# A cross-attention and maxout kernel: the order of its prologue, with state 1's small load and products placed later

## The chip, the cores and the metric

The kernel runs on one core of one Trainium2 chip. The metric is device time in microseconds (us) of one execution; lower is better. The kernel before takes 147.46 us (median of three runs, 147.34 to 148.67).

## The reference

Two parts follow each other. The first is attention between a sequence `x` (8 states in the batch, 8 heads, 512 rows, 64 columns) and a small `state` (32 rows per head), in both directions:

```python
scores = scale * x @ state.T ;  a = softmax(scores) ;  xread = a @ state
scores2 = scale * state @ x.T ; a2 = softmax(scores2); sread = a2 @ x
x = concat([xread, sread], axis=2)      # 544 rows per state, heads side by side: 512 columns
```

The second is a maxout layer over all 4352 rows: `g = maximum(x @ w1, x @ w2)`, `out = g @ w_out`, with `w1` and `w2` of 512 x 1024 and `w_out` of 1024 x 512, all in float32.

## The kernel before, in words

The work goes state by state (b = 0 to 7, one per batch element). The kernel uses `maximum(h1, h2) = h2 + relu(h1 - h2)`, so that it needs only the difference `wd` = W1 - W2 and the product `wwo` = W2 Wo. It also folds the state S into the weights: S (W1 - W2) and S W2 Wo together are a tile `sw` per state. The rows of one state are then `relu(a S (W1-W2)) Wo + a S W2 Wo`: "l1" (L348) multiplies `sw` with the transposed attention weights `aT` and takes relu, "l2" (L361, L366) multiplies the result with `wo` and adds the second term. All products are in bf16, so each float32 load is cast first.

From state 2 on, a loop (L550) issues the states one after another. All that comes before, states 0 and 1 with the load and preparation of the weights, is the prologue. Its order on every engine is written out by hand in the string `ORDER` (L18): tokens are read from left to right (L544), and each issues one step. Since every engine works through its own instructions in the order of issue, the string sets the queue of each engine. A token is of one of three kinds:

- A bare name is a DMA on SP's queue: `ldx.b.g` loads half of x of state b (512 KB, L134), `ldw1.q` and `ldw2.q` a quarter of W1 or W2 (512 KB, L145), `ldwo.f0.f1` two of eight rows of tiles of Wo (512 KB, L150), `ldS.lo.hi` states lo to hi (64 KB for one state, L155; state 0's load goes to ACT's queue instead, L451). `atd.b`, `xtd.b` and `std` are DMAs that transpose within the chip's memory: of the attention weights (L270), of x (L214) and of states 3 to 7 (L172). `store.b` writes an output.
- A name with `:n` is a group of matmuls of TensorE into PSUM bank n. `idle.9.512:7` issues nine matmuls on zeros (L446). `S.lo.hi` transposes the state (two transposes for one state, L176), `xt.b.k` a quarter of x (four, L219), `w2.q` a quarter of W2 (eight, L419), `at.b.g` half of the attention weights (four, L274). `sc.b.h` are scores (eight, L228), `sr.b` is the read of the state's side (32 small ones, L284), `ww.i.f0.f1` are two of the eight products of row i of W2 Wo (L439). `swh.b.z` is S times columns 512z to 512z + 511 of `wd` or `wwo` (eight, into two banks, L315). `sw` is the same for a quarter. `l1.b.f` are two matmuls (L348), `l2p` and `l2o` parts of l2 (L501, L505).
- A name with `>A`, `>V` or `>P` is a step of ScalarE (ACT), VectorE (DVE) or GpSimd (POOL). `cS`, `ce`, `cb`, `cw2`, `cwo` are casts of the state, of x (in two layouts), of W2 and of Wo (L160, L195, L201, L415, L436). `sub.q.k` is one eighth of W1 - W2 (L431). `cSm` are masked casts of states 2 to 7 (L165). `red` and `nm` sum and normalise (L250, L254). A name that also occurs as a matmul group moves that group's result out of PSUM, on lines 92 (ACT), 94 (DVE) and 96 (POOL), or 342 and 344 for relu.

A copy or cast helper has one line for all tiles, so an instruction is told by its tile. The float32 tiles `h` that loads write to rotate over ten buffers (L121). SP allows eight of its transfers to be under way; the next one waits for the one that was issued eight before it.

Of the kernel before, what the change touches and what calls it, by code (L numbers as in the profile page):

```python
# [15 lines left out]


ORDER = """  # L18
ldx.0.1 ldx.0.0 ldw2.1 ldwo.0.2 ldS.1.2 ldw2.0 ldw1.0 ldw1.1 ldwo.2.4 ldx.1.1 ldw2.3 ldw2.2 ldwo.4.6 ldwo.6.8
ldw1.2 ldw1.3 ldx.1.0 ldx.2.1 ldx.2.0 ldS.2.8 idle.9.512:7 cS.0.1>V ce.0.2>V S.0.1:0 S.0.1.0>A ce.0.3>P xt.0.2:1  # L20
S.0.1.1>A xt.0.2>V xt.0.3:7 ce.0.0>V ce.0.1>A xt.0.3>V xt.0.0:3 xt.0.1:4 xt.0.0>A sc.0.1:5 xt.0.1>V sc.0.1>A
sc.0.0:6 cw2.1>V sc.0.0>A red.0.1>V w2.1:2 sr.0:0 w2.1>A cwo.0>P red.0.0>V cS.1.2>A sr.0>V nm.0.1>P ww.2.0.2:1
cw2.0>A S.1.2:7 ww.3.0.2:3 nm.0.0>V S.1.2.0>A w2.0:4 S.1.2.1>A sub.0.0>V at.0.0:5 w2.0>A at.0.1:6 sub.0.1>V
sub.1.1>V at.0.0>A ww.1.0.2:2 ww.0.0.2:0 at.0.1>A sub.1.0>V cwo.1>V swh.0.0:7,4 swh.1.0:5,6 swh.0.0.1>A swh.0.0.0>V
ww.1.2.4:2 swh.1.0.1>A ww.0.2.4:0 swh.1.0.0>V l1.0.0:4 l1.0.3:7 l1.0.0>A l1.0.2:6 ce.1.2>V l1.0.1:5 ce.1.3>P
l1.0.3>V l1.0.2>A xt.1.2:4 ww.2.2.4:1 l1.0.1>A xt.1.2>V cw2.3>P xt.1.3:7 ww.3.2.4:3 xt.1.3>V l2p.0.1.0.2:6 w2.3:4
cw2.2>P sc.1.1:5 w2.3>V l2p.0.3.0.2:7 sc.1.1>A l2p.0.3.2.4:7 red.1.1>V w2.2:4 l2p.0.1.2.4:6 w2.2>A l2p.0.0.0.2:5
cwo.2>V l2p.0.0.2.4:5 nm.1.1>V cwo.3>A ww.2.4.6:1 ww.0.4.6:0 ww.3.4.6:3 sub.2.1>V ww.3.6.8:3 sub.2.0>V ww.0.6.8:0
ww.3>A ww.2.6.8:1 sub.3.1>V ww.0>A ww.1.4.6:2 ww.1.6.8:2 sub.3.0>V ww.2>A l2p.0.2.0.2:4 ww.1>A ce.1.0>V swh.0.1:3,0
ce.1.1>P l2p.0.2.2.4:4 swh.0.1.1>A swh.0.1.0>V xt.1.0:1 xt.1.1:2 xt.1.0>A l1.0.5:0 xt.1.1>V cb.2.1>P l1.0.4:3  # L30
l1.0.5>A sc.1.0:1 l1.0.4>V l1.0.6:2 ce.2.3>P sc.1.0>A l1.0.7:0 ce.2.1>P l1.0.6>A red.1.0>V l2p.0.0.4.6:5
l2p.0.1.4.6:6 ce.2.2>P l1.0.7>A sw.0.4:3,1 nm.1.0>P cSm.1>A l2p.0.3.4.6:7 sw.0.4.1>V l2p.0.0.6.8:5 l2p.0.1.6.8:6
sw.0.4.0>A ce.2.0>P atd.1 l2p.0.3.6.8:7 cSm.0>A cb.2.0>P l2o.0.1:6 swh.1.2:2,0 l2.0.1>V swh.1.1:1,3 xtd.2 std
ldx.3.0 ldx.3.1 swh.1.2.0>A l2o.0.3:7 swh.1.1.0>V S.2.3:6 swh.1.2.1>A l2o.0.0:5 S2>V l2p.0.2.4.6:4 l2.0.3>A
l2.0.0>V l2p.0.2.6.8:4 swh.1.1.1>A l1.1.2:2 l1.1.3:1 l1.1.2>V l1.1.0:0 l1.1.3>A l1.1.4:6 l1.1.0>A l1.1.7:7 l1.1.1:5
l1.1.4>A l1.1.7>V l1.1.5:3 l1.1.1>A l1.1.6:2 l1.1.5>V sc.2.0:1 l1.1.6>A sc.2.1:0 l2o.0.2:4 sc.2.0>A l2.1.0:6
sc.2.1>A red.2.0>V l2.0.2>A store.0 red.2.1>V nm.2.0>P l2.1.1:7 l2.1.0>A nm.2.1>P atd.2 l2.1.1>A
"""


# [688 lines left out]
```

## Time and profile before

| what | value |
|---|---|
| runs | 147.34, 147.46, 148.67 us |
| the execution that was profiled | 148.65 us |
| its span, from the first to the last instruction | 146.9 us |
| busy: TensorE, its weight loads, DVE, ACT, POOL | 137.7, 67.2, 80.0, 70.0, 47.6 us |
| read from memory and written to it | 15.20 MB, 8.91 MB |

A row of the timeline has the start in us from the span's start, the duration, the engine, the line, the operation, its output and inputs, their shapes and the number of instructions that were merged; the bracket gives the idle time of the engine before it and what ended it. PE is TensorE, PEld its weight loads, SPq the issue of a DMA by SP. Matmuls are pipelined: one of 512 columns has a duration of about 0.38 us, and the next starts 0.216 us after it, so a group of n takes n x 0.216 of TensorE's time. A row of stretches gives, for each, the busy time of PE, PEld, DVE, ACT and POOL with the number of instructions in parentheses, then the granted clock, the busy share of the DMA engines and GB/s. In the DMA view, q1 is the queue of the kernel's transfers and q8 one that fetches instructions; its share is that of 16 DMA engines over the stretch asked for.

### The profile page before, as it was taken

Reading aid. Unit: us, or ns where it says so; the run is one execution under the profiler, and the core shown is the slowest. Engines: PE = TensorE matmul, PEld = TensorE weight load, DVE = VectorE, ACT = ScalarE, POOL = GpSimd, SP = SyncE. Lnnn points to the kernel's source line nnn. Section 1 sums busy time; section 2 is a strip of 40 time slices with the busy share of each in tenths; the row PEclk is TensorE's granted clock in tenths of the full one; section 3 lists DMA queues with packets and bytes.
Section 4 is the critical chain, followed back from the end, with each engine's and each line's share of the span. In section 5 each row is a group of like instructions: output and inputs, shape, how many; then the busy total and the mean of one; then the engine's idle time right before and its main releaser. Section 6 shows DMA issues by size and latency. Waiting matters only on the chain. (4 is left out here: it accounts for less than half of the span.)

```text
span 146.9 us, 3048 instructions
## 1 busy us (share of the span) xinstructions
PE 137.7 (94%) x1218; PEld 67.2 (46%) x1218; DVE 80.0 (54%) x159; ACT 70.0 (48%) x133; POOL 47.6 (32%) x73
## 2 busy tenths in 40 slices
PE   6857599999999999999999999999999999999991
PEld 2444156453454445444544454454445344753451
DVE  1586568764663838463854585276637485720321
ACT  4388346687782556336541835181547145510200
POOL 4233060277008806464390457056500500000000
PEclk9999999999999999999999999999999999999998
DMA  4999999932999999996989685879307032400524
GB/s 106 334 375 388 367 389 370 331 61 47 200 266 350 185 270 355 152 230 261 184 167 267 274 165 113 269 286 147 71 2 288 0 71 107 185 9 9 189 97 143
DMA packets 36979, 29.68 MB, mean 202 GB/s; under 512 B 23904, under 2 KB 32352, under 8 KB 36064
## 3 DMA queue, kind: packets, MB, share of 16 engines
q1 hardware_dynamic: 36688, 29.36, 69.7%
q8 instruction: 11, 0.18, 0.5%
q10 hardware_dynamic: 272, 0.07, 0.2%
q14 instruction: 8, 0.07, 0.2%
HBM read 15.20 MB, written 8.91 MB: 164 GB/s over the span
## 5 line engine op out<-in xcount | busy, mean ns | idle before, releaser
L368 PE MATMUL bank<-wo,r 128*128 128x512 bf16 (+2 forms) x264 | 61.5, 373 | 0.1
L368 PEld LDWEIGHTS <-r 128*128 128x128 bf16 x264 | 25.4, 98 | 29.5 <-issue 1.1
L92 ACT COPY h<-bank 128x512 f32<-128x512 f32 (+1 forms) x17 | 9.7, 573 | 48.9 <-PE bank L368 48.9
L344 DVE TENSOR_SCALAR r<-bank 128x512 bf16<-128x512 f32 x29 | 20.1, 692 | 18.6 <-PE bank L353 18.1
L353 PE MATMUL bank<-aT,sw 128*128 128x512 bf16 x128 | 29.3, 379 | 0.0
L342 ACT ACTIVATE r<-bank 128x512 bf16<-128x512 f32 x35 | 20.7, 611 | 7.2 <-PE bank L353 6.7
L255 POOL TENSOR_TENSOR a<-e,er 128x512 bf16<-128x512 bf16 x14 | 14.9, 1082 | 26.7 <-ACT e L247 16.4
L94 DVE CAST sw<-bank 128x512 bf16<-128x512 f32 x23 | 14.7, 685 | 13.1 <-PE bank L323 13.1
L96 POOL CAST xe<-h 128x512 bf16<-128x512 f32 x27 | 16.2, 634 | 16.6 <-DMA h<-in_x_dram 14.4
L363 PE MATMUL bank<-sw,aT 128*128 128x512 bf16 (+2 forms) x66 | 19.1, 374 | 0.0
L96 POOL CAST xb<-h 128x1024 bf16<-128x1024 f32 x12 | 12.3, 1042 | 19.5 <-issue 12.5
L353 PEld LDWEIGHTS <-sw 128*128 128x128 bf16 x128 | 12.1, 98 | 13.7
L94 DVE COPY h<-bank 128x512 f32<-128x512 f32 (+1 forms) x16 | 10.5, 661 | 11.8 <-PE bank L368 10.2
L92 ACT CAST sw<-bank 128x512 bf16<-128x512 f32 x25 | 13.4, 600 | 2.0 <-PE bank L323 2.0
L251 DVE TENSOR_REDUCE sums<-e 128x16 f32<-128x512 bf16 x16 | 10.6, 664 | 2.5 <-ACT e L247 2.3
L441 PE MATMUL bank<-wo,w2t 128*128 128x512 bf16 x32 | 8.0, 379 | 3.3 <-DVE wo L94 1.7
L247 ACT ACTIVATE e<-bank 128x512 bf16<-128x512 f32 x16 | 8.9, 596 | 2.4 <-PE bank L239 1.8
L363 PEld LDWEIGHTS <-aT 128*128 128x128 bf16 x66 | 5.4, 98 | 5.0 <-issue 0.7
L239 PEld LDWEIGHTS <-xt 128*128 128x128 bf16 x128 | 5.0, 98 | 2.0 <-ACT xt L92 0.3
L433 DVE TENSOR_TENSOR wd<-h,h 128x512 bf16<-128x512 f32 x8 | 5.1, 688 | 1.3 <-DMA h<-in_moe_w_dram 1.3
L441 PEld LDWEIGHTS <-w2t 128*128 128x128 bf16 x32 | 2.9, 97 | 6.2 <-issue 2.1
L239 PE MATMUL bank<-sbd,xt 128*128 128x64 bf16 x128 | 5.4, 193 | 0.2 <-ACT xt L92 0.2
(75 smaller groups left out, 99.7 us busy)
## 6 DMA issues: line engine op xcount, KB each, us to landing
out_dram<-h SPq DMA_DIRECT2D x7, 1024.0 KB, 4.5
h<-in_x_dram SPq DMA_DIRECT2D x10, 512.0 KB, 5.3
h<-in_moe_w_dram SPq DMA_DIRECT2D x8, 512.0 KB, 10.3
h<-in_x_dram SPq DMA_DIRECT2D x3, 1024.0 KB, 5.8
h<-in_moe_w_out_dram SPq DMA_DIRECT2D x4, 512.0 KB, 11.5
out_dram<-h SPq DMA_DIRECT2D x3, 256.0 KB, 2.4
out_dram<-rs SPq DMA_DIRECT2D x2, 256.0 KB, 2.4
sf<-in_state_dram SPq DMA_DIRECT2D x1, 384.0 KB, 9.2
```

The source lines that it names most:

```text
L92: nc.scalar.copy(o, i)
L94: nc.vector.tensor_copy(o, i)
L96: nc.gpsimd.tensor_copy(o, i)
L239: nc.tensor.matmul(pv[:, c, kk], d["xt"][:, c, k, :], sbd[:, b, k, :], start=(c == 0 and kk == 0), stop=(c == NC - 1 and kk == 1))
L251: nc.vector.tensor_reduce(es_all[:, b, hh], e_view(b, hh), axis=AXX, op=ALU.add)
L255: (nc.gpsimd if eng == "P" else nc.vector).tensor_mul(e_view(b, hh, "a"), e_view(b, hh), d_(b)["er"][:, hh].unsqueeze(3).to_broadcast([128 ...
L342: nc.scalar.activation(out=o, in_=p, func=ACTF.Relu)
L344: nc.vector.tensor_scalar(o, p, scalar1=0.0, scalar2=None, op0=ALU.max)
L353: nc.tensor.matmul(p, SW[b][:, g, f * 128:(f + 1) * 128], AT[b][:, g].rearrange("p c t -> p (c t)"), start=(g == 0), stop=(g == 1))
L363: nc.tensor.matmul(p[:, lo:hi], AT[b][:, g, c, :], SW[b][:, g, FF + lo:FF + hi], start=(start and g == 0), stop=(stop and g == 1))
L368: nc.tensor.matmul(p[:, lo:hi], R[b][:, f, c * 128:(c + 1) * 128], wo[:, f, lo:hi], start=(start and j == 0), stop=(stop and j == len(fs) ...
L441: nc.tensor.matmul(p, w2t[:, f, i, :], wo[:, f, :], start=(f == 0), stop=(f == NF - 1))
```

## The change

Only `ORDER` differs. In the prologue's first part:

- `ldS.1.2` goes from behind `ldwo.0.2` to behind `ldwo.2.4` in SP's queue, so behind two quarters of W1, one of W2 and the second Wo piece. Its cast `cS.1.2`, its transposes `S.1.2` and the first group `swh.1.0` of state 1 move too: before, they were issued between the first ww groups and ahead of the second Wo piece's cast; now they follow it (`cwo.1>V swh.0.0 cS.1.2>A swh.0.0.0>A ... S.1.2:4 ww.3.2.4 ww.0.2.4 ... l1.0.1 swh.1.0`).
- `idle.9` becomes `idle.8`.
- The early casts and evictions change engines: `cS.0.1` from DVE to ACT, `ce.0.3` from POOL to DVE, `ce.0.0` from DVE to POOL, `ce.0.1` from ACT to DVE, `cw2.1` from DVE to POOL, `nm.0.1` from POOL to DVE; state 0's first scores `sc.0.1` go ahead of the transposes of x's other half.
- Banks and the order of the later groups change up to the prologue's end. `std` goes behind `ldx.3.0` and `ldx.3.1`, the masked casts `cSm` go from ACT to DVE, `nm.1.0` from POOL to DVE, and `S.2.3` from ahead of state 1's l1 groups to among them.

```diff
 ORDER = """
-ldx.0.1 ldx.0.0 ldw2.1 ldwo.0.2 ldS.1.2 ldw2.0 ldw1.0 ldw1.1 ldwo.2.4 ldx.1.1 ldw2.3 ldw2.2 ldwo.4.6 ldwo.6.8
-ldw1.2 ldw1.3 ldx.1.0 ldx.2.1 ldx.2.0 ldS.2.8 idle.9.512:7 cS.0.1>V ce.0.2>V S.0.1:0 S.0.1.0>A ce.0.3>P xt.0.2:1
-S.0.1.1>A xt.0.2>V xt.0.3:7 ce.0.0>V ce.0.1>A xt.0.3>V xt.0.0:3 xt.0.1:4 xt.0.0>A sc.0.1:5 xt.0.1>V sc.0.1>A
-sc.0.0:6 cw2.1>V sc.0.0>A red.0.1>V w2.1:2 sr.0:0 w2.1>A cwo.0>P red.0.0>V cS.1.2>A sr.0>V nm.0.1>P ww.2.0.2:1
-cw2.0>A S.1.2:7 ww.3.0.2:3 nm.0.0>V S.1.2.0>A w2.0:4 S.1.2.1>A sub.0.0>V at.0.0:5 w2.0>A at.0.1:6 sub.0.1>V
-sub.1.1>V at.0.0>A ww.1.0.2:2 ww.0.0.2:0 at.0.1>A sub.1.0>V cwo.1>V swh.0.0:7,4 swh.1.0:5,6 swh.0.0.1>A swh.0.0.0>V
-ww.1.2.4:2 swh.1.0.1>A ww.0.2.4:0 swh.1.0.0>V l1.0.0:4 l1.0.3:7 l1.0.0>A l1.0.2:6 ce.1.2>V l1.0.1:5 ce.1.3>P
-l1.0.3>V l1.0.2>A xt.1.2:4 ww.2.2.4:1 l1.0.1>A xt.1.2>V cw2.3>P xt.1.3:7 ww.3.2.4:3 xt.1.3>V l2p.0.1.0.2:6 w2.3:4
...
-l1.0.5>A sc.1.0:1 l1.0.4>V l1.0.6:2 ce.2.3>P sc.1.0>A l1.0.7:0 ce.2.1>P l1.0.6>A red.1.0>V l2p.0.0.4.6:5
-l2p.0.1.4.6:6 ce.2.2>P l1.0.7>A sw.0.4:3,1 nm.1.0>P cSm.1>A l2p.0.3.4.6:7 sw.0.4.1>V l2p.0.0.6.8:5 l2p.0.1.6.8:6
-sw.0.4.0>A ce.2.0>P atd.1 l2p.0.3.6.8:7 cSm.0>A cb.2.0>P l2o.0.1:6 swh.1.2:2,0 l2.0.1>V swh.1.1:1,3 xtd.2 std
-ldx.3.0 ldx.3.1 swh.1.2.0>A l2o.0.3:7 swh.1.1.0>V S.2.3:6 swh.1.2.1>A l2o.0.0:5 S2>V l2p.0.2.4.6:4 l2.0.3>A
...
+ldx.0.1 ldx.0.0 ldw2.1 ldwo.0.2 ldw2.0 ldw1.0 ldw1.1 ldwo.2.4 ldS.1.2 ldx.1.1 ldw2.3 ldw2.2 ldwo.4.6 ldwo.6.8
+ldw1.2 ldw1.3 ldx.1.0 ldx.2.1 ldx.2.0 ldS.2.8 idle.8.512:7 cS.0.1>A ce.0.2>V S.0.1:0 ce.0.3>V xt.0.2:1 S.0.1.0>V
+xt.0.3:2 xt.0.2>A S.0.1.1>V xt.0.3>V ce.0.0>P sc.0.1:6 ce.0.1>V xt.0.0:4 sc.0.1>A xt.0.1:7 xt.0.0>V xt.0.1>A
+red.0.1>V cw2.1>P sc.0.0:3 sc.0.0>A nm.0.1>V w2.1:5 sr.0:0 w2.1>A red.0.0>V cwo.0>P sr.0>V ww.2.0.2:1 cw2.0>A
+nm.0.0>V ww.3.0.2:2 at.0.1:6 w2.0:4 at.0.1>A sub.0.1>V at.0.0:7 w2.0>A sub.0.0>V sub.1.0>V at.0.0>A ww.1.0.2:3
+ww.0.0.2:5 sub.1.1>V cwo.1>V swh.0.0:0,6 cS.1.2>A swh.0.0.0>A swh.0.0.1>V S.1.2:4 ww.3.2.4:2 ww.0.2.4:5 S.1.2.0>V
+S.1.2.1>V l1.0.1:7 swh.1.0:0,6 l1.0.1>V l1.0.3:4 swh.1.0.0>A ww.1.2.4:3 ce.1.3>V swh.1.0.1>A l1.0.0:7 ce.1.2>P
+l1.0.3>A xt.1.3:0 l1.0.0>V ww.2.2.4:1 xt.1.3>A cw2.3>P xt.1.2:6 l1.0.2:4 xt.1.2>V l2p.0.0.0.2:7 l1.0.2>V sc.1.1:0
...
+swh.0.1:1,2 l2p.0.3.2.4:0 ce.1.0>P swh.0.1.0>A swh.0.1.1>V xt.1.1:5 xt.1.0:3 xt.1.1>A l1.0.5:1 xt.1.0>V cb.2.1>P
+l1.0.4:2 l1.0.5>A sc.1.0:5 l1.0.4>V l1.0.7:3 ce.2.3>P sc.1.0>A l1.0.6:1 ce.2.0>P l1.0.7>A red.1.0>V l2p.0.0.4.6:7
+l2p.0.2.4.6:4 ce.2.2>P l1.0.6>A swh.1.2:2,5 nm.1.0>V l2p.0.3.4.6:0 swh.1.2.0>A l2p.0.2.6.8:4 swh.1.2.1>V cb.2.0>P
+atd.1 l2p.0.3.6.8:0 cSm.0>V sw.0.4:3,1 swh.1.1:2,5 ce.2.1>P sw.0.4.0>A sw.0.4.1>V l2p.0.1.4.6:6 xtd.2 ldx.3.0
+ldx.3.1 l2p.0.1.6.8:6 swh.1.1.1>V l2o.0.1:6 l2o.0.3:0 swh.1.1.0>V l2.0.1>A l2p.0.0.6.8:7 l2.0.3>V l2o.0.0:7
+l1.1.2:3 cSm.1>V std l2.0.0>A l1.1.1:1 l1.1.2>A l1.1.6:5 l1.1.1>V l1.1.5:2 l1.1.6>A l1.1.0:6 l1.1.5>A l1.1.3:0
+l1.1.0>V S.2.3:7 l1.1.7:3 l1.1.3>A S2>V l1.1.4:1 l1.1.7>V sc.2.1:5 l1.1.4>A sc.2.0:2 l2o.0.2:4 sc.2.0>A l2.1.1:6
...
 """
```

More of the change, by code (lines that the diff above doesn't have):

```diff
@@ L24 @@
-sub.1.1>V at.0.0>A ww.1.0.2:2 ww.0.0.2:0 at.0.1>A sub.1.0>V cwo.1>V swh.0.0:7,4 swh.1.0:5,6 swh.0.0.1>A swh.0.0.0>V
-ww.1.2.4:2 swh.1.0.1>A ww.0.2.4:0 swh.1.0.0>V l1.0.0:4 l1.0.3:7 l1.0.0>A l1.0.2:6 ce.1.2>V l1.0.1:5 ce.1.3>P
-l1.0.3>V l1.0.2>A xt.1.2:4 ww.2.2.4:1 l1.0.1>A xt.1.2>V cw2.3>P xt.1.3:7 ww.3.2.4:3 xt.1.3>V l2p.0.1.0.2:6 w2.3:4
-cw2.2>P sc.1.1:5 w2.3>V l2p.0.3.0.2:7 sc.1.1>A l2p.0.3.2.4:7 red.1.1>V w2.2:4 l2p.0.1.2.4:6 w2.2>A l2p.0.0.0.2:5
-cwo.2>V l2p.0.0.2.4:5 nm.1.1>V cwo.3>A ww.2.4.6:1 ww.0.4.6:0 ww.3.4.6:3 sub.2.1>V ww.3.6.8:3 sub.2.0>V ww.0.6.8:0
@@ L29 @@
-ww.3>A ww.2.6.8:1 sub.3.1>V ww.0>A ww.1.4.6:2 ww.1.6.8:2 sub.3.0>V ww.2>A l2p.0.2.0.2:4 ww.1>A ce.1.0>V swh.0.1:3,0
-ce.1.1>P l2p.0.2.2.4:4 swh.0.1.1>A swh.0.1.0>V xt.1.0:1 xt.1.1:2 xt.1.0>A l1.0.5:0 xt.1.1>V cb.2.1>P l1.0.4:3
-l1.0.5>A sc.1.0:1 l1.0.4>V l1.0.6:2 ce.2.3>P sc.1.0>A l1.0.7:0 ce.2.1>P l1.0.6>A red.1.0>V l2p.0.0.4.6:5
-l2p.0.1.4.6:6 ce.2.2>P l1.0.7>A sw.0.4:3,1 nm.1.0>P cSm.1>A l2p.0.3.4.6:7 sw.0.4.1>V l2p.0.0.6.8:5 l2p.0.1.6.8:6
-sw.0.4.0>A ce.2.0>P atd.1 l2p.0.3.6.8:7 cSm.0>A cb.2.0>P l2o.0.1:6 swh.1.2:2,0 l2.0.1>V swh.1.1:1,3 xtd.2 std
@@ L34 @@
-ldx.3.0 ldx.3.1 swh.1.2.0>A l2o.0.3:7 swh.1.1.0>V S.2.3:6 swh.1.2.1>A l2o.0.0:5 S2>V l2p.0.2.4.6:4 l2.0.3>A
-l2.0.0>V l2p.0.2.6.8:4 swh.1.1.1>A l1.1.2:2 l1.1.3:1 l1.1.2>V l1.1.0:0 l1.1.3>A l1.1.4:6 l1.1.0>A l1.1.7:7 l1.1.1:5
-l1.1.4>A l1.1.7>V l1.1.5:3 l1.1.1>A l1.1.6:2 l1.1.5>V sc.2.0:1 l1.1.6>A sc.2.1:0 l2o.0.2:4 sc.2.0>A l2.1.0:6
-sc.2.1>A red.2.0>V l2.0.2>A store.0 red.2.1>V nm.2.0>P l2.1.1:7 l2.1.0>A nm.2.1>P atd.2 l2.1.1>A
+ldx.0.1 ldx.0.0 ldw2.1 ldwo.0.2 ldw2.0 ldw1.0 ldw1.1 ldwo.2.4 ldS.1.2 ldx.1.1 ldw2.3 ldw2.2 ldwo.4.6 ldwo.6.8
@@ new lines @@
+S.1.2.1>V l1.0.1:7 swh.1.0:0,6 l1.0.1>V l1.0.3:4 swh.1.0.0>A ww.1.2.4:3 ce.1.3>V swh.1.0.1>A l1.0.0:7 ce.1.2>P
+l1.0.3>A xt.1.3:0 l1.0.0>V ww.2.2.4:1 xt.1.3>A cw2.3>P xt.1.2:6 l1.0.2:4 xt.1.2>V l2p.0.0.0.2:7 l1.0.2>V sc.1.1:0
+w2.3:6 sc.1.1>A cw2.2>V l2p.0.0.2.4:7 w2.3>A red.1.1>V l2p.0.2.0.2:4 l2p.0.2.2.4:4 cwo.2>P w2.2:0 l2p.0.1.0.2:6
+w2.2>V nm.1.1>P ww.3.4.6:2 cwo.3>A ww.2.4.6:1 ww.1.4.6:3 ww.2.6.8:1 sub.2.1>V ww.3.6.8:2 ww.2>A l2p.0.1.2.4:6
+sub.2.0>V ww.3>A ww.0.4.6:5 sub.3.0>V ww.0.6.8:5 ww.1.6.8:3 sub.3.1>V ww.0>A l2p.0.3.0.2:0 ww.1>A ce.1.1>V
@@ L38 @@
+l1.1.2:3 cSm.1>V std l2.0.0>A l1.1.1:1 l1.1.2>A l1.1.6:5 l1.1.1>V l1.1.5:2 l1.1.6>A l1.1.0:6 l1.1.5>A l1.1.3:0
+l1.1.0>V S.2.3:7 l1.1.7:3 l1.1.3>A S2>V l1.1.4:1 l1.1.7>V sc.2.1:5 l1.1.4>A sc.2.0:2 l2o.0.2:4 sc.2.0>A l2.1.1:6
+l2.0.2>A store.0 red.2.0>V sc.2.1>A nm.2.0>P red.2.1>V l2.1.0:7 l2.1.1>A nm.2.1>P atd.2 l2.1.0>A
 """
```

## The prediction

> **What bounds the kernel now.** I read the page first, then TensorE's busy time by stretches, its waits, and the timeline of the first 30 us on all engines.
>
> ```profile
> PE 137.7 (94%) x1218; PEld 67.2 (46%) x1218; DVE 80.0 (54%) x159; ACT 70.0 (48%) x133; POOL 47.6 (32%) x73
> 0.00:20.00 20.00, 13.97 (x137) 7.03 (x138) 11.42 (x25) 10.87 (x20) 5.87 (x22) 1.00 0.93 321
> 20.00:50.00 30.00, 30.00 (x269) 14.39 (x268) 18.57 (x37) 20.08 (x35) 13.55 (x17) 1.00 0.86 238
> 50.00:100.00 50.00, 50.00 (x474) 23.79 (x473) 28.92 (x58) 24.54 (x50) 21.86 (x28) 1.00 0.90 229
> PE bank L441 <- DVE wo L94: 1.7, 1, 1.7
> ```
>
> TensorE (third column) is full from 20 us to 100 us and idle for 6.0 us of the first 20. So an edit can move the end in two ways only: by when TensorE last runs dry in the prologue and how much of its work is left then, or by a new wait later. Its longest wait is for the second Wo piece (wo.2.4). The timeline shows how it comes about:
>
> ```profile
> 1.19 4.02 PE L448 MATMUL bank<-wz 128*128 128x512 bf16 x9 [1.19 <-DVE ones L453]
> 2.85 0.59 SPq L156 DMA_DIRECT2D sf<-in_state_dram  x1
> 4.63 0.29 DVE L94 CAST sb<-sf 128x256 bf16<-128x256 f32 x1 [3.21 <-DMA sf<-in_state_dram]
> 4.95 0.87 POOL L96 CAST xe<-h 128x512 bf16<-128x512 f32 x1 [2.50 <-DMA h<-in_x_dram]
> 5.40 0.97 PE L222 MATMUL bank<-ident,xe 128*128 128x128 bf16 x8
> 5.46 0.53 ACT L92 COPY sbd<-bank 64x128 bf16<-64x128 bf16 x2 [2.71 <-PE bank L181]
> 6.41 0.62 ACT L92 CAST xe<-h 128x512 bf16<-128x512 f32 x1 [0.42 <-DMA h<-in_x_dram]
> 8.13 0.69 DVE L94 CAST w2b<-h 128x1024 bf16<-128x1024 f32 x1
> 9.54 1.01 ACT L92 COPY w2t<-bank 128x1024 bf16<-128x1024 bf16 x1 [0.48 <-PE bank L423]
> 9.68 1.04 POOL L96 CAST wo<-h 128x1024 bf16<-128x1024 f32 x1 [3.86 <-DMA h<-in_moe_w_out_dram]
> 10.44 0.41 ACT L92 CAST sb<-sf 128x256 bf16<-128x256 f32 x1
> 11.18 1.05 ACT L92 CAST w2b<-h 128x1024 bf16<-128x1024 f32 x1 [0.32 <-DMA h<-in_moe_w_dram]
> 11.20 0.27 PE L181 MATMUL bank<-ident,sb 128*128 128x128 bf16 x2
> 12.28 0.62 PE L423 MATMUL bank<-ident,w2b 128*128 128x128 bf16 x8 [0.38 <-ACT w2b L92]
> 12.61 2.58 DVE L433 TENSOR_TENSOR wd<-h,h 128x512 bf16<-128x512 f32 x4 [1.33 <-DMA h<-in_moe_w_dram]
> 12.94 1.01 ACT L92 COPY w2t<-bank 128x1024 bf16<-128x1024 bf16 x1 [0.28 <-PE bank L423]
> 14.00 1.04 PE L441 MATMUL bank<-wo,w2t 128*128 128x512 bf16 x4 [0.66 <-ACT w2t L92]
> 14.97 0.88 PE L323 MATMUL bank<-wd,sbd 64*32 64x512 bf16 x16
> 16.80 0.69 DVE L94 CAST wo<-h 128x1024 bf16<-128x1024 f32 x1 [1.61 <-DMA h<-in_moe_w_out_dram]
> 17.54 1.02 PE L441 MATMUL bank<-wo,w2t 128*128 128x512 bf16 x4 [1.69 <-DVE wo L94]
> 18.31 0.61 POOL L96 CAST xe<-h 128x512 bf16<-128x512 f32 x1 [6.13 <-DMA h<-in_x_dram]
> 18.40 1.89 PE L353 MATMUL bank<-aT,sw 128*128 128x512 bf16 x8
> 20.13 0.39 PE L222 MATMUL bank<-ident,xe 128*128 128x128 bf16 x4
> ```
>
> The casts that a DMA releases give the landings: w2.1 8.1, wo.0.2 9.7, w2.0 11.2, w1.0 12.6, w1.1 by 13.9 (the third subtraction follows without a gap), wo.2.4 16.8, x1.1 18.3. Each 512 KB takes about 1.4 us, but wo.2.4 comes 2.9 us after w1.1. The DMA view says why:
>
> ```profile
> DMA packets 36, 0.05 MB, mean 502 GB/s; under 512 B 4, under 2 KB 33, under 8 KB 35
> q8 instruction: 1, 0.02, 69.6%
> ...
> DMA packets 164, 0.17 MB, mean 336 GB/s; under 512 B 0, under 2 KB 164, under 8 KB 164
> ```
>
> The first two lines are 14.50 to 14.60 us: an instruction packet starts there (0.696 of a slice of 1.6 engine-us is 1.11 us on one engine). The third is 15.00 to 15.50: every packet is one of x1.1's 1 KB ones, none a 2 KB one of wo.2.4, which still hasn't landed. So fifteen engines were done with wo.2.4 by then and one held its last packets behind the instruction packet. On schedule it would have landed near 13.9 + 1.4 = 15.3; the collision costs 1.5. [...]
>
> **The base.** This execution took 148.65 us, its span 146.9 and 1.75 around it. The runs were 147.34, 147.46 and 148.67. Without the collision TensorE would resume at 15.3 + 0.69 + 0.05 = 16.04 (0.05 is the step from the cast's end, 16.80 + 0.69, to 17.54), 1.50 earlier; it would then reach x1's transposes at 20.13 - 1.50 = 18.63, while their cast ends at 18.31 + 0.61 + 0.05 = 18.97, and lose 0.34. That gives 148.65 - 1.50 + 0.34 = 147.5, the median. I take it that the median is a run without the collision and the profile one with it.
>
> **The change part by part.**
>
> Fillers and first transposes. Eight fillers end 0.42 us earlier ((4.02 - 0.63) / 8, the last one lasting 0.63). State 0's cast moves from DVE (0.29) to ACT (0.41), so TensorE starts its transposes at 5.09, not 5.00. The casts of x0 and the evictions change engines; the scores of x0's first half come 0.5 us earlier, those of its second half 0.65 later, because their cast goes to POOL (0.87 beside DVE, for 0.62 on ACT) and one eviction queues on ACT behind an exp. w2.1's cast on POOL (1.04 for 0.69) ends at 9.2, and its copy on ACT runs 9.9 to 10.9 instead of 9.54 to 10.55. All of this is hidden: the next link, ACT's cast of w2.0, waits for a landing at 11.
>
> Loads. S.1.2 passes w2.0, w1.0, w1.1 and wo.2.4 in SP's queue. Its share is what lies between wo.0.2 and w2.0, 11.18 - 9.68 = 1.50, over the usual 1.36 to 1.43 of one load: 0.07 to 0.14, and by its own landing
>
> ```profile
> DMA to landing us min/median/max: 3.9/7.0/9.2
> ```
>
> (issue 2.85, median 7.0, so 9.85) 0.17. I take 0.15 off those four loads; S.1.2 itself lands 0.17 behind wo.2.4.
>
> The chain with those numbers: w2.0 11.03; ACT's cast 1.05 to 12.08; transposes 12.13 to 12.75; ACT's copy to 13.80; ww.1.0.2 and ww.0.0.2 from 13.85 to 14.71 (four at 0.216, as eight take 1.89). DVE's four subtractions end 0.15 earlier, at 15.04, so swh.0.0's last pair issues at 15.09 and is through at 15.31. wo.2.4 lands at 15.15, DVE's cast ends at 15.84, ww.3.2.4 can start at 15.90. S.1.2 lands at 15.32, ACT's cast ends at 15.73, and its two transposes (0.11) run 15.78 to 15.90. ACT's eviction of swh.0.0 now queues behind that cast; it ends at 16.2, before l1.0.1 needs it at 16.76.
>
> So TensorE resumes at 15.90 with the same work left as before at 17.54, except swh.1.0, which before ran inside the wait and now comes after it: half of the 16 matmuls of 0.88, 0.44. 15.90 + 0.44 - 17.54 = -1.20.
>
> What is late next. TensorE now runs 1.2 us closer to loads that don't move. It reaches xt.1.3 at 15.90 + 6 x 0.43 + 0.44 = 18.92; its cast ends at 18.97: 0.05. The casts of the later Wo and W2 pieces, the subtractions and x1.0's cast follow their landings with slack of 0 to 0.1 by the same count; l1.0.5 waits 0.1 for DVE's eviction of swh.0.1. I take 0.15 in all, bounds 0 and 0.5 (the largest single slip being one cast on POOL instead of DVE, 1.04 for 0.69).
>
> State transposes behind x3.
>
> ```profile
> 10.60 0.68 DVE L255 TENSOR_TENSOR a<-e,er 128x512 bf16<-128x512 bf16 x1
> ...
> 33.18 0.95 ACT L168 ACTIVATE sb<-sf,zm 128x768 bf16<-128x768 f32 x1
> 33.48 1.05 POOL L255 TENSOR_TENSOR a<-e,er 128x512 bf16<-128x512 bf16 x1 [1.29 <-DVE er L252]
> ...
> 38.02 1.84 SPq L173 DMA_TRANSPOSE sbd<-sb  x1
> 39.91 1.29 SPq L140 DMA_DIRECT2D h<-in_x_dram  x2
> 56.15 0.63 PE L239 MATMUL bank<-sbd,xt 128*128 128x64 bf16 x16
> ```
>
> x3's issue moves up by the 1.9 us that SP spends on the state transposes, which then go some 3 us later. Their first user is state 3's scores at 56.15: over 10 us of cover; nothing. DVE takes nm.1.0 from POOL (0.68 for 1.05), the two state masks from ACT and the two evictions of each state's transposes. The last two the trace shows on ACT alone; on DVE they lie between half and one and a half times ACT's 0.95 and 0.53. All three move to an engine that is 54% busy, at places where TensorE has other groups queued that don't read them: nothing, and if that cover were gone up to 0.7 for a mask.
>
> Sum: 148.65 - 1.20 + 0.15 = **147.6**; against the median it is +0.1, since the run without the collision already has most of it.
>
> **The rivals.**
>
> Slower by the fetch. The instruction packet came between the third and fourth of the four matmuls at 14.00. The new order has three matmuls fewer before that place (a filler, S.1.2's two), so the same count falls into swh.0.0's first, from 14.71: the packet would start at 14.7 to 15.1, while wo.2.4's packets end near 14.5 and S.1.2's near 14.7. [...] If the packet starts before 14.7, wo.2.4 or S.1.2 lands 1.5 later. Now both gate TensorE: S.1.2 at 16.8, cast to 17.2, ww.3.2.4 at 17.37; 17.37 + 0.44 - 17.54 = +0.27, so 148.9.
>
> Slower by the clock. The nine fillers go at 0.42 us each, later ones at 0.216: TensorE starts at half rate, and the eight transposes at 5.40 are where it changes. With eight fillers it is idle for about 0.4 us before state 0's transposes. If the full rate then comes only after the prologue, the evictions of w2.1 shift ACT by about 0.85, w2.0's transposes cost 0.4, the two ww groups 0.84, swh.0.0 0.4, less 0.6 of slack to 15.90: up to 1.9; I take 1.5, so 149.1. [...] The trace agrees with a change after some 4.9 us.
>
> Faster. The profile with its collision is what the runs do too, and its 1.19 over the median lies around it. Then -1.05 counts against 147.46: 146.4. For it: only one of three runs was at 148.67. Against it: 147.5 came out of rows without that assumption.
>
> **How the numbers follow.** 0.46 for 147.6 (own range 147.2 to 148.2), 0.22 for the fetch, 0.14 for the clock, 0.18 for faster. A measurement of this kernel tells about 1% (1.5 us) from no change: 146.0 to 148.9. Slower: half of the fetch (0.11), most of the clock (0.13), 0.06 for waits that I didn't find: 0.30. Faster: under half of that case and a little of the first: 0.12. The range takes in both sides, 146.0 to 149.4.
>
> **What would show it.** Right: wo's second cast on DVE starts near 15.2 and the group of L441 after it near 15.9; TensorE is full from 19 on; the instruction packet starts after 14.7. Wrong: wo's cast near 16.7 or S.1.2's cast on ACT near 16.8 (fetch), matmuls at 0.42 after 6.3 us (clock), or new idle time of TensorE between 19 and 50 us, which no part of the sum has.

## The result and the profile after

The changed kernel takes 148.68 us (median of 20 runs, 148.19 to 150.44), the kernel before 147.49 us beside it (20 runs). The ratio of the times is 1.0081, with a 95% interval of 1.0058 to 1.0104: 0.8% slower, which is within the 1% that I took as no change. It is 1.1 over the forecast of 147.6, and that 1.1 has a cause, or rather two.

The profiled execution took 150.16, its span is 148.4. The page of the changed kernel, its rows of busy time and of the granted clock (40 slices of 3.7 us each, in tenths of full speed):

```profile
PE 141.2 (95%) x1217; PEld 68.5 (46%) x1217; DVE 84.1 (57%) x165; ACT 67.6 (46%) x127; POOL 47.0 (32%) x73
PEclk9975599999999999999999999999999999999999
```

TensorE is busy 3.5 us longer for the same work. The clock row says where: before it was 9 in all slices but the last, after it is 7, 5 and 5 in the third to fifth slice, from about 9 to 19 us. The stretches of the changed kernel, the three that were shown of before and then windows of 3.41 us (columns as before: length, PE, PEld, DVE, ACT, POOL, clock, DMA share, GB/s):

```profile
0.00:20.00 20.00, 16.07 (x122) 7.69 (x122) 10.86 (x25) 9.19 (x14) 5.39 (x22) 0.74 0.93 322
20.00:50.00 30.00, 30.00 (x275) 14.47 (x275) 21.75 (x37) 18.55 (x33) 12.19 (x15) 1.00 0.88 231
50.00:100.00 50.00, 50.00 (x471) 23.65 (x470) 29.18 (x60) 24.22 (x50) 23.05 (x30) 1.00 0.87 227
...
5.55:8.96 3.41, 2.41 (x32) 1.53 (x31) 2.99 (x9) 1.82 (x4) 1.53 (x2) 1.00 1.02 344
8.96:12.37 3.41, 2.69 (x43) 1.68 (x44) 2.58 (x6) 2.50 (x3) 1.19 (x2) 0.50 1.05 398
12.37:15.79 3.42, 2.74 (x19) 1.93 (x18) 3.11 (x5) 1.89 (x3) 0.00 (x0) 0.50 1.08 357
15.79:19.20 3.41, 3.41 (x17) 1.07 (x16) 0.98 (x3) 1.08 (x3) 0.61 (x1) 0.50 1.06 381
19.20:22.61 3.41, 3.41 (x29) 1.59 (x28) 1.78 (x4) 2.07 (x4) 1.48 (x2) 1.00 1.05 387
```

By the trace's clock records it is full from 5.55 on, for 3.41 us, falls to half at 8.96 and is full again at 19.20: 10.24 us, three times 3.41. From 20 us on TensorE never stands still, as in the kernel before; all that this execution loses, it loses in the prologue. The column does not show the slow start: it stands at 1.00 before 5.55 too, where the matmuls on zeros follow each other at (3.59 - 0.63) / 7 = 0.42 instead of 0.216 (first row of the next fence). The mean clock that each run lists leaves that start out in the same way. The same places of the timeline as in the prediction, now of the changed kernel:

```profile
1.19 3.59 PE L448 MATMUL bank<-wz 128*128 128x512 bf16 x8 [1.19 <-DVE ones L453]
5.45 0.73 PE L222 MATMUL bank<-ident,xe 128*128 128x128 bf16 x8
9.13 1.04 PE L423 MATMUL bank<-ident,w2b 128*128 128x128 bf16 x8 [0.26 <-POOL w2b L96]
11.28 1.89 PE L441 MATMUL bank<-wo,w2t 128*128 128x512 bf16 x4 [0.54 <-ACT w2t L92]
14.96 0.69 DVE L94 CAST wo<-h 128x1024 bf16<-128x1024 f32 x1
15.55 1.89 PE L441 MATMUL bank<-wo,w2t 128*128 128x512 bf16 x4 [0.68 <-ACT w2t L92]
15.87 0.42 ACT L92 CAST sb<-sf 128x256 bf16<-128x256 f32 x1
17.37 0.63 PE L323 MATMUL bank<-wd,sbd 64*32 64x512 bf16 x8
18.12 1.57 PE L441 MATMUL bank<-wo,w2t 128*128 128x512 bf16 x4
19.52 0.59 PE L353 MATMUL bank<-aT,sw 128*128 128x512 bf16 x2
```

Eight transposes of x take 0.73 at 5.45 (0.97 at 5.40 in the kernel before, where the clock record begins at 6.13), so the full rate came no later than before. Eight transposes of W2 take 1.04 at 9.13 (0.62 in the kernel before), and four ww matmuls 1.89 instead of 1.04. Wo's cast starts at 14.96, earlier than I had said: the load that it waits for lands 1.84 earlier than in the profile before. But TensorE comes to the group behind it only at 18.12 (forecast 15.90) and, at half rate until 19.20, to the first l1 at 19.52 (forecast 15.90 + 4 x 0.216 = 16.76): 2.76 late. The forecast span, 147.6 - 1.75 = 145.85, plus 2.76 makes 148.6; measured 148.4.

The DMA view of the changed kernel, 15.70 to 15.90 us:

```profile
q8 instruction: 1, 0.02, 35.7%
```

The instruction packet comes there, behind wo.2.4, and not into it.

So the clock explains the profiled execution. It does not explain all runs. A half-rate window of 3.41 us is 1.2% of the mean clock that each run lists. Of the 20 runs three have a mean clock of 0.965 or 0.966 (three windows; 150.16 to 150.44), six have 0.977 (two windows; 148.61 to 149.31), and eleven have 0.987 or more. Seven of these eleven have lost one window (0.987 or 0.988), four none. They take 148.19 to 148.29 alike, two of them 148.75: still 0.6 over the forecast. No profile of the changed kernel itself shows such a run.

### The profile page after: what moved, and what is told of

Its sections match the earlier page's. It is cut to its first block, busy times and chain, and to the rows that moved or that the text cites. A ratio compares the mean times of both kernels' runs of the same rounds, so it can differ in the third digit from the quotient of the medians.

```text
span 148.4 us, 3047 instructions
## 1 busy us (share of the span) xinstructions
PE 141.2 (95%) x1217; PEld 68.5 (46%) x1217; DVE 84.1 (57%) x165; ACT 67.6 (46%) x127; POOL 47.0 (32%) x73
## 5 line engine op out<-in xcount | busy, mean ns | idle before, releaser
L92 ACT COPY h<-bank 128x512 f32<-128x512 f32 (+1 forms) x18 | 10.3, 572 | 50.8 <-PE bank L368 45.5
L344 DVE TENSOR_SCALAR r<-bank 128x512 bf16<-128x512 f32 x31 | 21.4, 692 | 19.2 <-PE bank L353 18.6
L353 PE MATMUL bank<-aT,sw 128*128 128x512 bf16 x128 | 29.9, 379 | 0.0
L94 DVE CAST sw<-bank 128x512 bf16<-128x512 f32 x24 | 15.3, 685 | 15.2 <-PE bank L323 15.2
L255 POOL TENSOR_TENSOR a<-e,er 128x512 bf16<-128x512 bf16 x13 | 13.4, 1049 | 31.5 <-ACT e L247 16.7
L342 ACT ACTIVATE r<-bank 128x512 bf16<-128x512 f32 x33 | 19.8, 613 | 4.0 <-PE bank L353 3.7
L94 DVE COPY h<-bank 128x512 f32<-128x512 f32 (+1 forms) x15 | 9.8, 661 | 10.3 <-PE bank L368 10.2
L92 ACT CAST sw<-bank 128x512 bf16<-128x512 f32 x24 | 12.8, 600 | 5.5 <-PE bank L323 5.5
L441 PE MATMUL bank<-wo,w2t 128*128 128x512 bf16 x32 | 10.3, 461 | 1.2 <-ACT w2t L92 1.2
```

What stands on the lines that cost most here:

```text
L92: nc.scalar.copy(o, i)
L94: nc.vector.tensor_copy(o, i)
L255: (nc.gpsimd if eng == "P" else nc.vector).tensor_mul(e_view(b, hh, "a"), e_view(b, hh), d_(b)["er"][:, hh].unsqueeze(3).to_broadcast([128 ...
L342: nc.scalar.activation(out=o, in_=p, func=ACTF.Relu)
L344: nc.vector.tensor_scalar(o, p, scalar1=0.0, scalar2=None, op0=ALU.max)
L353: nc.tensor.matmul(p, SW[b][:, g, f * 128:(f + 1) * 128], AT[b][:, g].rearrange("p c t -> p (c t)"), start=(g == 0), stop=(g == 1))
```

## The experiments

Two questions: where the clock goes and what it costs, and what the 0.6 is that stays where the clock is lost for one window or not at all. For the first, one theory has it that the missing ninth filler loses the clock, the other that state 1's move does, by the gaps that it leaves in TensorE's work. For the second, the theory at the start was a wait that the sum doesn't have, with the steps that went to DVE behind it; the rival, that the move itself costs more than it was given. The names in parentheses are those by which the expectations name other runs.

**The changed order with nine fillers (e1_after9).** Only the filler count goes back.

```diff
-idle.8.512:7 cS.0.1>A
+idle.9.512:7 cS.0.1>A
```

> The changed kernel with nine fillers instead of eight. Theory C (the changed kernel is slower because TensorE drops to half rate in the prologue, and the missing filler brings that about): the granted clock shows no half-rate windows (mean 0.99 to 1.0 instead of 0.965 to 0.988) and the time is 148.2 us or less. Theory M (it is slower because swh.1.0 and S.1.2 now stand between the second Wo piece and the rest): the time stays near 148.2 to 148.7, whatever the clock. If the half-rate windows come from the reordered steps and not from the filler, they stay too.

Measured: 148.22 (12 runs, 147.22 to 149.15), ratio 1.0035 (1.0007 to 1.0063). Of the twelve runs one has a mean clock of 0.977, five have 0.985 to 0.988 and six 0.997 or more, where the changed kernel with eight fillers has 0.977 or less in nine of 20. So the ninth filler makes the longer losses rarer. The profiled execution kept the full clock, so it shows the changed order as I had costed it. Its timeline:

```profile
15.24 0.69 DVE L94 CAST wo<-h 128x1024 bf16<-128x1024 f32 x1
15.45 0.40 ACT L92 CAST sb<-sf 128x256 bf16<-128x256 f32 x1 [1.14 <-DMA sf<-in_state_dram]
15.91 0.29 PE L181 MATMUL bank<-ident,sb 128*128 128x128 bf16 x2 [0.32 <-ACT sb L92]
16.03 1.03 PE L441 MATMUL bank<-wo,w2t 128*128 128x512 bf16 x4
18.22 0.88 POOL L96 CAST xe<-h 128x512 bf16<-128x512 f32 x1 [7.41 <-DMA h<-in_x_dram]
19.07 0.39 PE L222 MATMUL bank<-ident,xe 128*128 128x128 bf16 x4
32.05 1.04 POOL L96 CAST xb<-h 128x1024 bf16<-128x1024 f32 x1
32.23 1.40 DVE L255 TENSOR_TENSOR a<-e,er 128x512 bf16<-128x512 bf16 x1
33.71 1.35 SPq L271 DMA_TRANSPOSE aT<-a  x1
35.25 2.72 SPq L216 DMA_TRANSPOSE xt<-xb  x1
37.94 0.38 PE L353 MATMUL bank<-aT,sw 128*128 128x512 bf16 x1 [0.55 <-DMA aT<-a]
```

The first six rows are the forecast almost to the digit: Wo's cast 15.24 (15.15), the state's cast 15.45 (15.32), ww.3.2.4 at 16.03 (15.90), xt.1.3 at 19.07 (18.97). The last five show what the forecast has not: state 1's attention weights are normalised on DVE (`nm.1.0`) in 1.40 us instead of 0.68, beside a cast on POOL; the transposing DMA `aT` lands at 37.89, 4.18 after its issue; and TensorE stands still for 0.55 at the first l1 of state 1. Other runs of this kernel, 147.22 to 147.39 (three) against 148.02 and up (nine), look as if they had the wait or had it not; the profiled one took 148.31.

**The kernel before with eight fillers (e2_before8).** The reverse edit.

```diff
-idle.9.512:7 cS.0.1>V
+idle.8.512:7 cS.0.1>V
```

> The kernel before with eight fillers instead of nine, nothing else. Theory C with the filler as the cause: half-rate windows appear in some runs, mean clock 0.965 to 0.988, time 148.0 to 149.5. Theory M, or theory C with the order as the cause: same as before within 0.2 us, 147.3 to 147.7.

Measured: 147.75 (12 runs, 147.38 to 148.65), 1.0019 (1.0000 to 1.0038). Five runs have a mean clock of 0.977 and lie at 147.69 to 147.93; six of the seven at full clock lie at 147.38 to 147.81. With nine fillers, beside it, two of 35 runs have 0.977 or less. One filler fewer thus loses the clock more often, also in the old order, where it costs some 0.3. The profiled execution has neither the loss nor the collision, and it tests the base of the prediction. Its timeline:

```profile
15.25 0.69 DVE L94 CAST wo<-h 128x1024 bf16<-128x1024 f32 x1
15.99 1.02 PE L441 MATMUL bank<-wo,w2t 128*128 128x512 bf16 x4
16.77 0.61 POOL L96 CAST xe<-h 128x512 bf16<-128x512 f32 x1 [4.64 <-DMA h<-in_x_dram]
19.55 1.04 POOL L96 CAST w2b<-h 128x1024 bf16<-128x1024 f32 x1 [2.17 <-DMA h<-in_moe_w_dram]
```

Forecast for before without its collision: 16.04. The last two rows show what "without" means. TensorE's packet starts at 16.22 here, and the load that it meets is w2.3, which lands 2.8 us behind x1.1 instead of 1.4. So this execution has the collision as well, two loads later, where less hangs on it.

**State 1's move alone, in the kernel before (e3_move),** and **the changed kernel without it (e4_undo).** In the first, the load, cast, transposes and `swh.1.0` move as in the change; the banks of some groups had to change with them, and `l1.0.3` and `ww.2.2.4` have other places. In the second they go back, also with other banks. The edits are shown in part.

```diff
-ldS.1.2 ldw2.0 ldw1.0 ldw1.1 ldwo.2.4 ldx.1.1
+ldw2.0 ldw1.0 ldw1.1 ldwo.2.4 ldS.1.2 ldx.1.1
...
-swh.0.0:7,4 swh.1.0:5,6 swh.0.0.1>A swh.0.0.0>V ww.1.2.4:2
+swh.0.0:7,4 cS.1.2>A swh.0.0.1>A swh.0.0.0>V S.1.2:5 ww.1.2.4:2
```

The second:

```diff
-ldw2.0 ldw1.0 ldw1.1 ldwo.2.4 ldS.1.2 ldx.1.1
+ldS.1.2 ldw2.0 ldw1.0 ldw1.1 ldwo.2.4 ldx.1.1
...
-swh.0.0:0,6 cS.1.2>A swh.0.0.0>A swh.0.0.1>V S.1.2:4 ww.3.2.4:2
+swh.0.0:0,6 swh.1.0:4,7 swh.0.0.0>A swh.0.0.1>V ww.3.2.4:2
```

> The kernel before with the state 1 part of the change alone: its load behind the second Wo piece, its cast, transposes and first S.(W1-W2) group behind that piece's cast; engines, fillers and the rest as before. Theory M: 0.3 to 0.8 us slower than before (the sum of the prediction gives +0.1 to +0.3 against a run without a collision). Theory C: same as before within 0.2 us and a clock as before.

> The changed kernel with its state 1 part put back: load, cast, transposes and first S.(W1-W2) group of state 1 early, both swh groups ahead of the second Wo piece; eight fillers, engines and later order as changed. Theory M: the fastest runs return to about 147.5. Theory C: half-rate windows stay (mean clock 0.965 to 0.988 in most runs) and the median stays 148.2 to 148.8.

Measured: 148.05 (11 runs), 1.0040 (1.0023 to 1.0056), all but one at full clock; and 148.34 (12 runs, 147.32 to 150.12), 1.0055 (1.0027 to 1.0084), with seven runs at 0.977 or less. So the clock is not lost by state 1's move but by the rest of the prologue with its eight fillers. By the times alone, both runs side with theory M: the first is 0.58 slower, and the second has runs at 147.32 and 147.49. The profiles speak against it. The first kernel's 0.58 is mostly a stall of my own bank order; TensorE's waits of it:

```profile
PE bank L353 <- DVE r L344: 0.5, 1, 0.5
```

0.45 of it is one stall at 19.44, which the profiles of the two orders don't have; a run with other banks was not made. What stays for the move, 0.1, is less than the run can tell. In the second kernel aT lands in time (below), so it does not tell the move from what follows.

**nm.1.0 back on GpSimd, in the changed kernel (e5_nmP).**

```diff
-swh.1.2:2,5 nm.1.0>V l2p.0.3.4.6:0
+swh.1.2:2,5 nm.1.0>P l2p.0.3.4.6:0
```

> The changed kernel with nm.1.0 (the normalising of state 1's second half) back on POOL; nothing else. Theory A (a new wait: state 1's transposed weights aT come late, because nm.1.0 on DVE takes 1.40 us beside POOL's cast instead of 0.68, and TensorE is idle before state 1's l1 for 0.55 us): the wait before l1 of state 1 is gone or under 0.2 us and the fastest runs fall from 148.2 to 147.4 to 147.7. Theory C (clock alone): unchanged, fastest runs 148.2, median 148.7. The clock is not touched, so under both theories most runs keep half-rate windows.

Measured: 148.92 (6 runs, 147.89 to 149.36), 1.0096 (1.0064 to 1.0129), two of them at 0.977. aT is issued earlier, at 33.21, but lands at 37.46, and TensorE still waits 0.44 for it. DVE's slow step was not the cause of that wait, or not all of it. Two more runs, 148.82 and 149.09, have 0.988 and 0.999, and no profile shows what they lost.

**The changed order, kept warm (e6_warm).** Seven more matmuls on zeros go into the gaps of the prologue, in banks that are free.

```diff
-ce.0.0>P sc.0.1:6
+ce.0.0>P idle.1.512:5 sc.0.1:6
-xt.0.1:7 xt.0.0>V
+xt.0.1:7 idle.1.512:5 xt.0.0>V
-sc.0.0:3 sc.0.0>A
+sc.0.0:3 idle.1.512:5 sc.0.0>A
-sr.0:0 w2.1>A
+sr.0:0 idle.2.512:4 w2.1>A
-at.0.0:7 w2.0>A
+at.0.0:7 idle.2.512:5 w2.0>A
```

> The changed kernel with seven more matmuls on zeros put into TensorE's gaps between 6 and 14 us (1, 1, 1, 2, 2), each 0.216 us at full rate, no other edit. Theory C: no half-rate windows after the first (mean clock 0.997 to 1.0 in nearly all runs), no run above 148.5, median 148.2 (that of the runs without such windows). Theory A alone: the median stays at 148.6 to 148.8 since the wait for aT is not touched. If short matmuls don't decide the clock, mean clocks stay 0.965 to 0.988.

Measured: 148.10 (12 runs), 1.0021 (0.9996 to 1.0045). All runs have a mean clock of 0.998 or more, and none is over 148.25: the clock theory holds, and the clock is worth 148.68 - 148.10 = 0.58 of the median. (Why it falls without them is another matter, and stays open.) The runs fall into two groups, 147.24 to 147.38 (four) and 148.01 to 148.25 (eight). None of the changed kernel's 20 runs is in the first, so a little of the 0.58 is that group; against the second group's median, 148.16, it is 0.52. The profiled execution is of the first. Its timeline:

```profile
32.04 0.69 DVE L255 TENSOR_TENSOR a<-e,er 128x512 bf16<-128x512 bf16 x1
32.05 1.58 POOL L96 CAST xb<-h 128x1024 bf16<-128x1024 f32 x1
32.81 1.35 SPq L271 DMA_TRANSPOSE aT<-a  x1
34.34 2.89 SPq L216 DMA_TRANSPOSE xt<-xb  x1
36.94 1.24 PE L353 MATMUL bank<-aT,sw 128*128 128x512 bf16 x5
```

Here `nm.1.0` takes 0.69 and the cast on POOL pays, aT is issued 0.9 earlier than in the run with nine fillers, and its landing at 36.90 is just in time. It is as slow as there, though: 4.09 after the issue.

**Both: warm, with nm.1.0 on GpSimd (e7_both),** and **the kernel before with nm.1.0 on DVE (e8_nmV).** The first has the last two edits together; the second:

```diff
-nm.1.0>P cSm.1>A
+nm.1.0>V cSm.1>A
```

> Both edits: nm.1.0 on POOL and the seven more matmuls on zeros. Theories A and C together: 147.3 to 147.6, as the kernel before, and a clock of 0.997 to 1.0. What is left over 147.47 is the price of the moved state 1 part, by the prediction's sum +0.1.

> The kernel before with nm.1.0 on DVE, as the changed kernel has it; nothing else. Theory A: aT is issued later or little earlier than before, since DVE needs 1.4 us beside POOL; TensorE waits up to 0.5 us before state 1's l1 in some runs: 147.5 to 148.0. Theory C: same as before within 0.1 us.

Measured: 147.93 (147.77 to 148.39), 1.0038 (1.0020 to 1.0056); and 147.41, 0.9992 (0.9976 to 1.0009). In the medians the engine of `nm.1.0` is worth at most 0.2, in the new order and in the old. In the first kernel TensorE waits as long as before. Its timeline:

```profile
33.25 1.35 SPq L271 DMA_TRANSPOSE aT<-a  x1
34.80 2.54 SPq L216 DMA_TRANSPOSE xt<-xb  x1
37.51 0.81 PE L353 MATMUL bank<-aT,sw 128*128 128x512 bf16 x3 [0.40 <-DMA aT<-a]
```

So the question became why aT takes 4.0 to 4.25 us in some kernels and 3.3 to 3.4 in others. The DMA records have the answer. Beside the 16 KB packets of q8, of which the first nine come once in 216 to 316 of TensorE's matmuls and weight loads in the kernel before and once in 163 to 321 in the changed one, there are 8 KB instruction packets on another queue, q14. Where the first of them in the span falls, and what aT does:

| kernel | aT issued | landed | took | first q14 packet |
|---|---|---|---|---|
| before | 34.56 | 37.92 | 3.36 | 44.73 |
| before, eight fillers | 33.35 | 36.73 | 3.38 | 43.29 |
| before, state 1 moved | 33.96 | 37.32 | 3.36 | 31.59 |
| before, nm.1.0 on DVE | 33.10 | 36.48 | 3.38 | 43.21 |
| changed, state 1 back | 35.62 | 38.97 | 3.35 | 41.08 |
| changed | 35.64 | 39.65 | 4.01 | 38.38 |
| changed, nine fillers | 33.71 | 37.89 | 4.18 | 36.52 |
| changed, nm.1.0 on POOL | 33.21 | 37.46 | 4.25 | 36.16 |
| changed, warm | 32.81 | 36.90 | 4.09 | 35.56 |
| changed, warm, nm.1.0 on POOL | 33.25 | 37.47 | 4.22 | 36.16 |

Where it comes 2.7 to 2.95 us after aT's issue, aT is late; elsewhere it is not. When it comes, VectorE has started 63 to 66 of its records in all of these but the third (52 there). So a count of VectorE's instructions nearly fits, and the change gives VectorE more to do: two masks, `nm.1.0`, evictions. That the packet is VectorE's is a guess so far.

**Moving the packet (e9_dve8).** The warm kernel, with VectorE's memset of `sbd` for two states issued nine times instead of once, from 1.1 us on, where VectorE has nothing to do for 3.6 us. Nothing else changes: not SP's order, not the masks.

```diff
-    nc.vector.memset(sbd[:, 0:2], 0.0)
+    for j in range(9):
+        nc.vector.memset(sbd[:, 0:2], 0.0)
```

> e6_warm with VectorE's 2-byte-column memset of sbd issued nine times instead of once (eight more tiny instructions at 1.1 us, where VectorE waits for data anyway). In every changed order so far an 8 KB instruction packet (queue q14) comes as VectorE issues its record 63 or 64, which is 2.7 to 2.9 us after the issue of the second batch's attention transpose (aT), and aT lands 4.0 to 4.2 us after its issue; in the orders where that packet falls elsewhere it lands after 3.4. Theory F (the packet delays aT): the packet now comes eight VectorE instructions earlier, near 31.7 us, while the DMA engines are idle; aT lands 3.4 us after its issue, the issue of xt's transpose on SP takes 1.8 instead of 2.5 to 2.9, and the slower group of runs (148.0 to 148.25) falls by 0.5 to 0.7: median 147.2 to 147.6. Theory O (x3's loads behind xt's transpose on SP, or the masks on VectorE, slow the transposes): aT still takes 4.0 to 4.2, median 148.1.

Measured: 147.51 (11 runs, 147.26 to 147.89), 0.9996 (0.9976 to 1.0017). The slower group is gone, and the median falls by 0.59. The DMA view of the warm kernel, 32 to 40 us, without the memsets:

```profile
q14 instruction: 1, 0.01, 0.5%
...
aT<-a SPq DMA_TRANSPOSE x1, 4.1
```

The same view and stretch with them:

```profile
q1 hardware_dynamic: 3424, 1.08, 65.2%
...
aT<-a SPq DMA_TRANSPOSE x1, 3.3
```

There is no q14 row any more (the packet came at 30.99, as VectorE had started 62 records, with the eight memsets among them), and aT takes 3.3. Its timeline:

```profile
1.15 3.40 DVE L456 MEMSET sbd<- 128x256 uint32 x9
32.45 1.07 DVE L255 TENSOR_TENSOR a<-e,er 128x512 bf16<-128x512 bf16 x1
33.61 1.35 SPq L271 DMA_TRANSPOSE aT<-a  x1
35.14 1.78 SPq L216 DMA_TRANSPOSE xt<-xb  x1
37.34 1.03 PE L353 MATMUL bank<-aT,sw 128*128 128x512 bf16 x3
```

xt's issue takes SP 1.78 instead of 2.89, and TensorE starts state 1's l1 without a wait, though DVE was slow again (1.07). The memsets are not as tiny as the expectation says: each writes 256 words per partition and the nine take 3.40, but they end at 4.55, before VectorE's first cast of x. This execution took 147.73; it started at half rate until 9.34, which its mean clock of 1.0 does not show.

The two groups of the warm kernel can now be read. aT came late in its profiled execution too, and cost nothing at 147.32, because `nm.1.0` took 0.69; with nine fillers it took 1.40, and the execution was at 148.31. By that reading, a late packet and a slow step on VectorE together cost 0.86, from the first group's median, 147.30, to the second's, 148.16; without the packet the slow step (1.07) is covered. That the step's length separates the groups is read from two profiles, and was not tested.

**The same memsets with nm.1.0 on GpSimd (e11_P_dve8).**

```diff
-nm.1.0>V
+nm.1.0>P
```

> e7_both (GpSimd does nm.1.0) with the same eight more tiny memsets. Theory F: aT lands 3.4 us after its issue at 33.2, so at 36.6 instead of 37.46, TensorE's wait of 0.40 for it is gone, and with nm.1.0 off VectorE there is no slower group left: 147.4 to 147.6, all runs within 0.3. Theory O: 147.9 as e7_both, wait 0.40.

Measured: 147.42 (147.18 to 147.93, and one of twelve runs at 150.49), 0.9994 (0.9972 to 1.0016). aT is issued at 33.24 and lands at 36.61; no wait. This is the best form of the changed order, and it is no better than the kernel before (147.44 beside it).

**Into the way, in the kernel before (e10_bef10, e12_bef6).** The reverse: ten, and then six more memsets there.

```diff
-    nc.vector.memset(sbd[:, 0:2], 0.0)
+    for j in range(11):
+        nc.vector.memset(sbd[:, 0:2], 0.0)
```

> The kernel before with ten more of those tiny memsets on VectorE (sbd's memset eleven times). Theory F: the 8 KB packet moves from 43 to 45 us to VectorE's record 53 or 54, some 2 us after aT's issue; aT lands 4.0 to 4.2 us after its issue instead of 3.4, about 0.3 behind the end of TensorE's other work there: 147.7 to 147.8 against 147.47, with a wait of TensorE's L353 for aT of about 0.3. Theory O: nothing changes, aT 3.4 and 147.4 to 147.5.

> The kernel before with six more of VectorE's tiny memsets (sbd's memset seven times). With ten more, VectorE's packet came at 30.8 us, ahead of aT's transpose; with none it comes near 43.2. Six more should put it near VectorE's record 53 to 57 of the kernel before, 34.8 to 37.7 us, while the second batch's attention transpose (issue near 33.4) is under way. Theory F: if the packet comes 2 to 3 us after aT's issue, aT lands 4.0 to 4.2 us after its issue instead of 3.4, TensorE's L353 waits some 0.3 for it, and the time is 147.7 to 147.8; if it misses that window, aT takes 3.4 and the time is 147.4 to 147.5, and the run says nothing. Theory O: aT takes 3.4 wherever the packet falls.

Measured: 147.49, 1.0007 (0.9988 to 1.0026), and 147.47, 1.0007 (0.9991 to 1.0024). Both missed. The packet came at 30.82 and at 32.03, ahead of aT's transfer, aT took 3.3 and 3.35, and the runs say nothing of the question, save that the packet moves with VectorE's instructions and that the count alone doesn't place it: 60 and 56 records had started, where 64 was the count without the memsets. The second, by chance, was profiled with the collision of the prediction's base. The DMA view of its 14.50 to 14.60 us:

```profile
q8 instruction: 1, 0.02, 69.6%
```

And its timeline:

```profile
16.80 0.69 DVE L94 CAST wo<-h 128x1024 bf16<-128x1024 f32 x1 [1.52 <-DMA h<-in_moe_w_out_dram]
```

These are the rows of the kernel before. That execution took 148.65, in a kernel whose median is 147.47; two of its twelve runs are there.

## Why the prediction was right, and where it failed

- **The verdict.** No change that stands clear of 1% was forecast, and 0.8% was measured, inside 146.0 to 149.4. That is a matter of the range's width. The sum's own range, 147.2 to 148.2, does not hold the 148.68, and nothing in the sum has the two losses; that they came to less than 1% at the median is luck, since three of the 20 runs are 1.8 to 2.0% slower.
- **The base** (the profile with a collision, the median without): right for TensorE, which resumes at 15.99 without it (forecast 16.04), and for the time. The collided execution is the rare one: one of the 20 runs of the kernel before is there (148.67), and the profiled one of the last kernel (148.65). But the packet is not absent otherwise; it meets a later load. So x1.1 was not bound to land near 18.3: in the kernel before with eight fillers its cast starts at 16.77, and the 0.34 that the base lost there is not lost.
- **The chain from the loads to 15.90:** right, within 0.13 in the execution with nine fillers and 0.07 in the warm one (15.83), both with more fillers than the sum had. The whole gain of the move is what the median already had, as the sum said.
- **The 0.15 for "what is late next", with bounds of 0 to 0.5:** this step failed. In its own stretch it holds (xt.1.3 0.10 late), in part by luck: x1.1 is late for another reason than in the profile before, since the packet now meets it (below). But the sum looked at TensorE's next waits up to 20 us and gave "nothing" to what moves to VectorE behind that, "an engine that is 54% busy, at places where TensorE has other groups queued". The step mis-sized is there: 0.59 at the median of the warm kernel, by an instruction packet that comes 2.7 to 2.95 us behind aT's issue and moves away when VectorE gets more instructions. The 0.68 for `nm.1.0` was wrong as well (up to 1.40 beside POOL); its engine is worth at most 0.2 in the medians. The prediction said that new idle time of TensorE between 19 and 50 us would show it wrong, and three profiled executions have it (0.55 with nine fillers, 0.44 and 0.40 with `nm.1.0` on POOL). The changed kernel's own profile has not: aT is late there too (4.01), but TensorE, still behind by the lost clock, comes to it only at 39.74, behind the landing at 39.65.
- **The rival of the fetch:** the mechanism was right and the packet wrong. TensorE's packet came after 14.7 (at 15.81, and at 15.50 with nine fillers), and missed wo.2.4 and S.1.2. It met the next load instead: with nine fillers x1.1's cast starts at 18.22, 2.8 behind the state's at 15.45. The packet on q14 hit aT.
- **The rival of the clock:** it was given 0.14 and 149.1, and nine of 20 runs have two or three half-rate windows, at 148.61 to 150.44. Its place was wrong: the full rate came in time, at 5.55, and was lost again at 8.96. Why it was lost no run shows; TensorE was busy for 2.41 of the 3.41 us ahead of the fall.
- **The states' transposes behind x3:** nothing, as said. The run with more memsets has the same order on SP and no wait.

The sum as measured, from the median: 148.68, less 0.58 (clock) and 0.59 (the packet on q14), is 147.51 against the forecast 147.6. (The two differences were taken one after the other, so they meet the last kernel's median by construction; that it lies at the kernel before's 147.44 is the finding.) The change itself is worth nothing, and the two losses come from things that it displaces.

Open: why TensorE's clock falls in the window from 5.55. Busy time doesn't tell it: the kernel before with eight fillers had only 2.16 of 3.41 in its window from 5.33, and kept the clock. Nor does the place of the window: the kernel before with `nm.1.0` on DVE reaches full rate at 5.41 and keeps it, the changed kernel at 5.55 and loses it. Open too is how one packet of 0.3 to 0.6 us on one queue holds aT for 0.7; what is shown is that moving it takes the delay away. That it delays aT in the old order wasn't shown, since both tries missed. What places the packet is open as well: in the five kernels where it comes ahead of aT (state 1 moved, and the four with more memsets) it comes at 30.6 to 32.0 us, as VectorE has started 52 to 62 records.
